# Moving the top three bits of a 64-bit weight's low word from a VectorE shift to a ScalarE byte read

## The chip, the cores and the metric

The kernel runs on one core of one Trainium2 chip. The metric is the device time of one execution in microseconds. Before the change the median of three runs is 1188.74 us (1188.38 to 1191.08). The engines are TensorE (PE; PEld is its weight load), VectorE (DVE), ScalarE (ACT), GpSimd (POOL) and SyncE (SP), which issues nearly all DMAs.

## The reference, cut to what matters

Windowed attention with memory tokens on 4 x 768 tokens, then two feed-forward layers on its 3072 x 512 output:

```python
# attention: chunks of 32 queries, 16 keys to the left, 8 to the right, 8 memory keys, 8 heads of 64
x = attention(q, k, v, mem_k, mem_v)          # (3072, 512)
# first layer: w_in 512 x 2048, w_out 2048 x 512
h = x @ w_in
P = a[0] + a[1]*h + a[2]*h**2 + a[3]*h**3
Q = 1 + abs(b[0])*abs(h) + abs(b[1])*h**2
x = (P / (Q + 1e-6)) @ w_out
# second layer: w1, w2 512 x 1024, w3 1024 x 1024, w_out 1024 x 512
return ((x @ w1) * (x @ w2) @ w3) @ w_out
```

All weights of the two layers arrive as 64-bit floats. A matmul here takes operands of a shorter format, so every weight and every activation is split into a high and a low part, and each product is made of three matmuls (high x high, high x low, low x high).

## The kernel before, in words

Tokens are processed in blocks of 384 (8 blocks). In the **first layer** a step n is one block and one of 16 slices of 128 hidden columns: twelve matmuls into a PSUM bank `h` (`gemm1`, three such banks), the rational function on ScalarE, VectorE and GpSimd (`rat_*`, lines 332 to 372), its split into `gh` (ScalarE) and `gl` (GpSimd, line 381), and twelve matmuls into four accumulators (`gemm2`). The last rational step, `rat_end` (line 372, VectorE), is what frees the bank `h`. Attention units of 64 queries run in between: scores on PE, softmax on VectorE, ScalarE and GpSimd (the normalisation, line 294), two more PE steps, and the split of the result into `xr`. The first six units, those of block 0, run before the first `gemm1`.

In the **second layer**, `gemm3` makes the two factors `ab` (w1 and w2, kept interleaved in `w12`), a gate multiplies and splits them, and w3 @ w_out is made once as eight products `w3o` (24 matmuls each), whose split results are the weights of `gemm4`. The eight `w3o` stand between the gated products of the first block.

**The decode.** Each of 72 weight chunks (128 x 512 values of 64 bits) is loaded into one of four buffers `raw`, as pairs of 32-bit words (low, high), and turned into a 32-bit float and its two parts by six steps (lines 204 to 240):

1. `load` (SP): the DMA, 512 KB.
2. `scale` (ScalarE, line 214): the high word, read as a float, times 2^-112, which moves its exponent to the 32-bit format's.
3. `low` (VectorE, line 218): the low word shifted right by 29, which leaves its top three bits.
4. `join`, twice (VectorE, line 222): the scaled word shifted left by three, or-ed with these bits; then or-ed with the sign.
5. `high_part` (ScalarE, line 226) into `wA` or `wB`, or into a buffer for w3.
6. `low_part` (GpSimd, line 229): the value less its high part. It and step 5 free the buffer.

32 chunks (w_in, w_out) are decoded in the ramp, that is until all slices of block 0 are done; 40 more (16 of w12, 8 of the second w_out, 16 of w3) from the last block of the first layer on, as their places come free.

**What sets the order.** Every step has a due time and, for each engine that may do it, a cost, both tables of numbers in the kernel (`R`, `DI`, `DO`, `DW`, `A0`, `AS`, `H0` and so on). A planner in the kernel (`order`, line 104) walks through a model of the engines and emits each engine's instructions in one fixed order; GpSimd's steps and those VectorE steps marked `port` never overlap in its model. On the chip every engine works in that order, and waits at the head of its queue for what the next instruction needs.

Of the kernel before, what the change touches and what calls it, by code (L numbers as in the profile page):

```python
# [26 lines left out]
NF1 = F1 // P  # L27
# [7 lines left out]
SIGN = -2 ** 31  # L35
# [3 lines left out]
def attention_rational_mlp_gated_mlp(  # L39
# [15 lines left out]
    pe, act, dve, pool, sp = nc.tensor, nc.scalar, nc.vector, nc.gpsimd, nc.sync  # L55
# [11 lines left out]
    wB = const.tile([P, NF1, 2, DM], F32R, name="wB")  # L67
# [6 lines left out]
    att = ExitStack()  # L74
# [7 lines left out]
    def bank(tag, name):  # L82
        return ps.tile([P, DM], F32, tag=tag, bufs=rings[tag], name=name)
# [111 lines left out]
    def raw(name):  # L195
        return rawp.tile([P, DM, 2], I32, tag="raw", name=name)

# [3 lines left out]

    def decode(t, src, dst, *ready, take=(), early=(), LOW=None):

        r, d = [], []

        def load():
            r.append(raw("w64"))
            sp.dma_start(out=r[0], in_=src.bitcast(I32).rearrange("p (k t) -> p k t", t=2))  # L210

        def scale():
            hi = r[0][:, :, 1].bitcast(F32)
            act.activation(out=hi, in_=hi, func=AF.Copy, scale=2.0 ** -112)  # L214

        def low():
            lo = r[0][:, :, 0]
            dve.tensor_scalar(out=lo, in0=lo, scalar1=29, scalar2=None, op0=ALU.logical_shift_right)  # L218

        def join(op, n):  # L220
            lo, hi = r[0][:, :, 0], r[0][:, :, 1]
            dve.scalar_tensor_tensor(out=lo, in0=hi, scalar=n, in1=lo, op0=op, op1=ALU.bitwise_or)  # L222

        def high_part():
            d.append(dst() if callable(dst) else dst)
            act.activation(out=d[0][:, 0], in_=r[0][:, :, 0].bitcast(F32), func=AF.Copy)

        def low_part(eng):
            eng.tensor_tensor(out=d[0][:, 1], in0=r[0][:, :, 0].bitcast(F32), in1=d[0][:, 0].bitcast(F32),  # L229
                              op=ALU.subtract)  # L230

        a = step(t, {"dma": 1.46}, load, *early, take=("raw",))
        b = step(t, {"act": 0.58}, scale, a)
        c = step(t, {"dve": 0.335}, low, a, port=True)
        c = step(t, {"dve": 0.602}, lambda: join(ALU.logical_shift_left, 3), b, c, port=True)
        c = step(t, {"dve": 0.602}, lambda: join(ALU.bitwise_and, SIGN), c, port=True)
        h = step(t + H0, {"act": 0.58}, high_part, c, *ready, take=take)
        l = step(t + H0, LOW or LOWA, low_part, h, frees=[a], port=True)
        a.until.append(h)
        return h, l  # L240

    def mm3(out_, w, wi, x, xi, first, last):

        for i, (a, c) in enumerate(((0, 0), (0, 1), (1, 0))):
            pe.matmul(out_, lhsT=wi(w, a), rhs=xi(x, c), start=first and i == 0, stop=last and i == 2)  # L245
# [185 lines left out]

    def w3o(i):

        o = w3os[i] = bank(("acc3", "att")[i % 2], "w3o")
        for jc in range(NF2):
            mm3(o, w3s[i, jc // 4], lambda w, a: w[:, a, jc % 4 * P:(jc % 4 + 1) * P], wB, lambda w, a: w[:, jc, a],
                jc == 0, jc == NF2 - 1)
# [52 lines left out]
    def wA_slot(f):  # L490
        return wA[:, f].rearrange("p a c k -> p a (c k)")

    def two(v, p, d):
        return {g: c for g, c in (("pool", p), ("dve", d)) if g[0] in v}

    PAIR7 = two('d', .551, .27); LOWB = two('p', 1.225, .602); GLO7 = two('p', .956, .469); GATE = two('p', .956, .469)
    LOWA, PAIR, GLO, XLO = two('p', 1.225, .602), two('p', .551, .27), two('p', .956, .469), two('d', 1.764, .87)
    H0 = 1.098
    FIN = {"act": 0.48, "dve": 0.6}

    def start():
# [8 lines left out]
    n1, n2 = NB * NF1, NB * NF2  # L510
    first = step(-99, {"none": 0.0}, start)
    G1, G2, VL = {}, {}, {}
    T0 = -9.693; UP = 0.781; A0 = -1.160; AS = 0.526


    lq, lv, s_, ex, tc_, v_ = ({-2: None, -1: None} for _ in range(6))
# [2 lines left out]
    def attend(u):  # L519
        blk, o = divmod(u, UPB)  # L520
        t = T0 + UP * u if blk == 0 else 8 / 3 * (u - UPB) + A0
        k = UP / 4 if blk == 0 else AS
# [16 lines left out]
        VL[u] = step(t + 1.55 * k, {"dve": 0.335}, lambda: v_parts(u, 1), vh, frees=[v_[u]])  # L539


    R = (0.00,0.64,0.28,0.40,0.44,0.36,0.64,0.52,0.83,0.81,1.11,1.39,1.21,1.59)
    DI, DO = -3.895, -2.305
    WI, WO = {}, {}
    chunks = sorted([(f + DI, 0, f) for f in range(NF1)] + [(f + LAG + 0.45 + DO, 1, f) for f in range(NF1)])
    SPL = {}

    def ffn1(n):
        blk, f = divmod(n, NF1)
        d = [VL[u] for u in range(blk * UPB, blk * UPB + UPB)] if f == 0 else [G1[n - 1]]  # L550
# [22 lines left out]

    for u in range(UPB):
        attend(u)
    for t, o, f in chunks:
        (WO if o else WI)[f] = decode(t, *((w_out[f], wB[:, f]) if o else (w_in[f], wA_slot(f))))
    u = UPB
    for n in range(n1):
        ffn1(n)  # L580
# [10 lines left out]
    sec = step(n1 - 16, {"none": 0.0}, second, *VL.values(), v_[NU - 1], tc_[NU - 1])  # L591
# [3 lines left out]
    tG = [n1 + m + 0.05 if m < LAG else TB + TG * (m - LAG) for m in range(NF2)]  # L595
    TW = TB + (NF2 - LAG) * TG + XB * TG
    tO = [TW + (TO + (TO + TM) * (i - 1) if i else 0) for i in range(NF2)]
    T1 = tO[-1] + TO
    PB = 1.23
    tG += [(TW + TG * (m - NF2 - XB) if m - NF2 < XB else T1 + PB * (m - NF2 - XB)) for m in range(NF2, n2)]  # L600
    DW, D3, DV = -2.122, -5.330, -1.521
    W12, WO2, W3, OP, G3, G4, X2 = {}, {}, {}, {}, {}, {}, {}
    for f in range(NF1):
        W12[f] = decode(tG[f // 2] + f % 2 * 0.4 + DW, w12[f], wA_slot(f), G1[n1 - NF1 + f], early=[G1[n1 - NF1 + max(0, f - 1)]], LOW={"dve": .602} if f < 0 else LOWB)
    for j in range(NF2):
        WO2[j] = decode(tO[0] + DV + 0.3 * j, w_out2[j], wB[:, j], G2[n1 - NF1 + j], early=[G2[n1 - NF1 + j]], LOW=LOWB)

    def x2(blk):
        t = tG[blk * NF2]
# [43 lines left out]
        gates[m] = ffn2_in(m)  # L653
    O = {}
    for i in range(NF2):
        W3[i] = [decode(tO[i] + 0.5 * g + D3, w3T[i, :, g], w3_dst(i, g), sec, take=("w3",), early=[sec] if i < 2 else [O[i - 2]], LOW=LOWB) for g in range(2)]
        t = tO[i]
        tag = ("acc3", "att")[i % 2]
        o = O[i] = step(t, {"pe": 5.61}, lambda i=i: w3o(i), *[x for p in W3[i] for x in p], *[x for p in WO2.values() for x in p],
                 G2[n1 - 1], *([G4[i - 2]] if i > 1 else []), take=(tag,), frees=[p[0] for p in W3[i]])  # L660
        d = []
        if i:
            ffn2_out(i - 1, t + TO)
            d = [G4[i - 1]]
# [78 lines left out]
```

## Time and profile before

| | |
|---|---|
| median of the runs | 1188.74 us |
| profiled execution, its own time | 1193.64 us |
| its span | 1191.8 us |
| PE busy | 1121.2 us (94%) |
| VectorE busy | 668.2 us (56%) |
| ScalarE busy | 667.0 us (56%) |
| GpSimd busy | 476.4 us (40%) |
| mean granted TensorE clock | 0.983 |

The profile is of one execution; its own time is the span plus what lies around it. Busy shares are averages over the whole: the page's slices and the tables by stage show where PE is not full, and the lists of waits show what ended its idle time there. The granted clock is TensorE's, as a share of its full 2.4 GHz; its lower level is 1.2 GHz.

### The profile page before, as it was taken

What the parts mean: (1) busy time and instruction counts of PE and PEld (TensorE: products, weight loads), DVE (VectorE), ACT (ScalarE), POOL (GpSimd) and SP (SyncE); (2) the same over time, 40 slices, a digit from 0 to 9 for tenths busy, and PEclk for the clock granted to TensorE, in tenths of its full rate; (3) what the DMA queues carried; (4) which work ended last, traced back from release to release, by engine and by line L of the source; (5) the groups of instructions that cost most, each with busy time, mean ns of one, the idle gap of its engine ahead of it and who ended that gap; (6) DMA issues with size and microseconds to landing.
All of it is one profiled execution on the core that took longest, in us unless ns stands there. A gap on an engine that the chain in (4) does not pass through costs nothing.

```text
span 1191.8 us, 18531 instructions
## 1 busy us (share of the span) xinstructions
PE 1121.2 (94%) x7104; PEld 1042.2 (87%) x7104; DVE 668.2 (56%) x1249; ACT 667.0 (56%) x1267; POOL 476.4 (40%) x444
## 2 busy tenths in 40 slices
PE   5587699999999999999999799989999999999998
PEld 4476589999999999999999699978889999999997
DVE  6799896667776677676767878855301010110100
ACT  4576687777787777777777866543312222222121
POOL 2466665444444444444444556633211111111111
PEclk9988799999999999999999999989999999999999
DMA  8535322121121121211220232643101101011000
GB/s 241 153 89 167 107 89 63 37 69 37 47 63 36 43 66 44 62 37 43 74 95 1 76 123 84 210 137 107 36 27 54 53 1 53 1 53 54 1 27 27
DMA packets 28028, 83.07 MB, mean 70 GB/s; under 512 B 3746, under 2 KB 3874, under 8 KB 27938
## 3 DMA queue, kind: packets, MB, share of 16 engines
q1 hardware_dynamic: 27648, 81.80, 22.1%
q8 instruction: 56, 0.92, 0.3%
q14 instruction: 32, 0.26, 0.1%
q10 hardware_dynamic: 292, 0.09, 0.0%
HBM read 69.30 MB, written 12.58 MB: 69 GB/s over the span
## 4 chain that ended last, share of the span: by engine, by line
PE 76%; DVE 7%; DMA 5%; ACT 5%; POOL 4%; issue 3%; SPq 0%; POOLq 0%; DVEq 0%; ACTq 0%
PE acc L245 28%; PE ab L245 19%; PE h L245 18%; PE w3o L245 4%; PE sc L262 3%; DVE w L222 2%; DMA w<-in_w_dram 2%; PE xo L308 2%; POOL wA L229 2%; DMA w<-in_w_in_dram 2%; DMA w<-in_w_out_dram 2%; PE at L299 1%; DVE w L218 1%; POOL wB L229 1%; ACT A L334 1%
## 5 line engine op out<-in xcount | busy, mean ns | idle before, releaser
L245 PE MATMUL h<-xr,wA 128*128 128x384 f32 x1536 | 308.7, 351 | 27.9 <-DVE A L372 26.7
L245 PEld LDWEIGHTS h<-xr,wA 128*128 128x128 f32 x1536 | 277.6, 195 | 35.6 <-DVE A L372 30.8
L245 PE MATMUL acc<-gh,wB 128*128 128x384 f32 x1024 | 287.4, 343 | 1.5 <-POOL wB L229 1.5
L245 PE MATMUL ab<-xr,wA 128*128 128x384 f32 x1536 | 280.1, 337 | 5.0 <-DVE W L460 4.5
L245 PEld LDWEIGHTS ab<-xr,wA 128*128 128x128 f32 x1536 | 271.2, 189 | 10.8 <-DVE W L460 5.1
L346 POOL TENSOR_TENSOR W<-W,Q 128x384 f32<-128x384 f32 x128 | 132.9, 1038 | 211.1 <-ACT Q L342 172.6
L460 DVE TENSOR_TENSOR W<-W,ab 128x384 f32<-128x384 f32 x64 | 35.4, 553 | 288.7 <-PE ab L245 287.5
L245 PEld LDWEIGHTS acc<-gh,wB 128*128 128x128 f32 x1024 | 186.2, 188 | 7.4 <-POOL wB L229 2.3
L245 PE MATMUL acc<-gl,wB 128*128 128x384 f32 x512 | 171.7, 335 | 0.0
L469 POOL TENSOR_TENSOR gl<-W,gh 128x384 fp32r<-128x384 f32 x56 | 56.8, 1016 | 280.4 <-ACT gh L464 280.4
L381 POOL TENSOR_TENSOR gl<-A,gh 128x384 fp32r<-128x384 f32 x128 | 136.7, 1069 | 41.1 <-ACT gh L376 33.9
L364 DVE SCALAR_TENSOR_TENSOR A<-A,cf,h 128x384 f32<-128x384 f32 x128 | 78.0, 609 | 102.4 <-ACT h L360 101.8
L222 DVE SCALAR_TENSOR_TENSOR w<-w 128x512 int32<-128x512 int32 x144 | 119.7, 854 | 5.9 <-ACT w L214 5.3
L456 ACT COPY W<-ab 128x384 f32<-128x384 f32 x64 | 30.7, 480 | 142.8 <-PE ab L245 142.8
L334 ACT ACTIVATE A<-h,cf 128x384 f32<-128x384 f32 x128 | 85.5, 668 | 43.0 <-PE h L245 42.3
L358 ACT ACTIVATE Q<-W,one 128x384 f32<-128x384 f32 x128 | 78.9, 616 | 41.0 <-POOL W L346 40.5
L245 PEld LDWEIGHTS acc<-gl,wB 128*128 128x128 f32 x512 | 96.4, 188 | 0.0
L464 ACT CAST gh<-W 128x384 fp32r<-128x384 f32 x56 | 28.7, 512 | 117.2 <-DVE W L460 110.7
L342 ACT ACTIVATE Q<-W,cf 128x384 f32<-128x384 f32 x128 | 90.8, 709 | 4.0
L245 PE MATMUL acc<-wB,gh 128*128 128x512 f32 x294 | 92.2, 394 | 0.0
L351 DVE TENSOR_TENSOR A<-A,h 128x384 f32<-128x384 f32 x128 | 70.1, 548 | 15.9 <-ACT W L334 14.2
L353 DVE SCALAR_TENSOR_TENSOR A<-A,cf,h 128x384 f32<-128x384 f32 x128 | 77.7, 607 | 2.3 <-ACT W L334 0.6
(61 smaller groups left out, 1401.4 us busy)
## 6 DMA issues: line engine op xcount, KB each, us to landing
qk<-in_qkT_dram SPq DMA_DIRECT2D x48, 320.0 KB, 3.9
w<-in_w_out_dram SPq DMA_DIRECT2D x24, 512.0 KB, 4.5
v<-in_vW_dram SPq DMA_DIRECT2D x48, 192.0 KB, 2.4
w<-in_w_in_dram SPq DMA_DIRECT2D x16, 512.0 KB, 4.8
w<-in_w3T_dram SPq DMA_DIRECT2D x16, 512.0 KB, 3.8
w<-in_w_dram SPq DMA_DIRECT2D x16, 512.0 KB, 4.5
x2d<-x2o SPq DMA_DIRECT2D x16, 384.0 KB, 2.7
x<-x2d SPq DMA_DIRECT2D x16, 384.0 KB, 4.1
```

The lines of the kernel that those rows point to most:

```text
L222: dve.scalar_tensor_tensor(out=lo, in0=hi, scalar=n, in1=lo, op0=op, op1=ALU.bitwise_or)
L229: eng.tensor_tensor(out=d[0][:, 1], in0=r[0][:, :, 0].bitcast(F32), in1=d[0][:, 0].bitcast(F32), op=ALU.subtract)
L245: pe.matmul(out_, lhsT=wi(w, a), rhs=xi(x, c), start=first and i == 0, stop=last and i == 2)
L334: act.activation(out=t, in_=hps[n][src], func=func, scale=scale, bias=bias)
L342: act.activation(out=t, in_=hps[n]["W"], func=AF.Identity, scale=cf[:, 5:6], bias=cf[:, 4:5])
L346: pool.tensor_tensor(out=W, in0=W, in1=Q, op=ALU.mult)
L351: dve.tensor_tensor(out=A, in0=A, in1=h, op=ALU.mult)
L353: dve.scalar_tensor_tensor(out=A, in0=A, scalar=cf[:, 1:2], in1=h, op0=ALU.add, op1=ALU.mult)
L358: act.activation(out=Q, in_=W, func=AF.Ln, bias=one)
L364: dve.scalar_tensor_tensor(out=A, in0=A, scalar=cf[:, 0:1], in1=r, op0=ALU.add, op1=ALU.mult)
L381: eng.tensor_tensor(out=gl, in0=hps.pop(n)["A"], in1=gt[n].bitcast(F32), op=ALU.subtract)
L469: eng.tensor_tensor(out=gl, in0=hps.pop(m), in1=gt[m].bitcast(F32), op=ALU.subtract)
```

## The change

In `decode`, step 3 can be done by ScalarE (`byte=True`): it reads only the top byte of the low word (one byte out of every eight), multiplies by 1/32, subtracts 0.484375 and writes an integer, whose rounding gives the same three bits. All 32 chunks of the ramp do this (`BYTE`), and every second one of the 40 later ones (`BYTT`). `w3o` puts all eight products into the bank `acc3` instead of alternating between `acc3` and `att`. Some due times are other numbers. The new arguments `tag`, `TAGS`, `TAGT` (a PSUM bank for the scaled word) are `None` everywhere, so nothing goes that way, and `LOWS`, `LOWT` name the same engine as before.

```diff
-        def low():
+        def low(eng):
             lo = r[0][:, :, 0]
-            dve.tensor_scalar(out=lo, in0=lo, scalar1=29, scalar2=None, op0=ALU.logical_shift_right)
+            if eng is act:
+                top = r[0].bitcast(U8).rearrange("p k (t b) -> p k t b", b=4)[:, :, 0, 3]
+                act.activation(out=lo, in_=top, func=AF.Copy, scale=1.0 / 32, bias=-0.484375)
+            else:
+                dve.tensor_scalar(out=lo, in0=lo, scalar1=29, scalar2=None, op0=ALU.logical_shift_right)
...
-        c = step(t, {"dve": 0.335}, low, a, port=True)
+        c = step(t, {"act": 0.58} if byte else {"dve": 0.335}, low, a, port=not byte)
...
-        o = w3os[i] = bank(("acc3", "att")[i % 2], "w3o")
+        o = w3os[i] = bank("acc3", "w3o")
...
-    H0 = 1.098
+    H0 = 1.034
+    TAGS, BYTE, LOWS = (None,), (True,), (LOWA,)
+    TAGT, BYTT, LOWT = (None,), (False, True), (LOWA,)
...
-    T0 = -9.693; UP = 0.781; A0 = -1.160; AS = 0.526
+    T0 = -9.693; UP = 0.781; A0 = -1.044; AS = 0.832
...
-    DI, DO = -3.895, -2.305
+    DI, DO = -4.925, -2.305
...
-    DW, D3, DV = -2.122, -5.330, -1.521
+    DW, D3, DV = -1.654, -5.330, -1.521
```

In `R`, the due time of `rat_slope` goes from 0.28 to 0.20. What stands in each engine's queue shows what moves.

VectorE in the ramp, in front of the `rat_end` (A<-h,A) of the first slice, for which the fourth `gemm1` waits; `w_...` are the decode's buffers, `e` and `r` the softmax's. Before:

```order
L353 SCALAR_TENSOR_TENSOR A<-A,cf,h 128x384
L276 TENSOR_TENSOR e_84<-sc,mx 128x384
L222 SCALAR_TENSOR_TENSOR w_409<-w_409 128x512
L218 TENSOR_SCALAR w_413<-w_413 128x512
L218 TENSOR_SCALAR w_418<-w_418 128x512
L284 TENSOR_REDUCE sm<-e_84 128x4
L364 SCALAR_TENSOR_TENSOR A<-A,cf,h 128x384
L288 TENSOR_SCALAR r<-sm 128x4
L289 RECIPROCAL r<-r 128x4
L368 SCALAR_TENSOR_TENSOR h<-W,one,h 128x384
L351 TENSOR_TENSOR A<-A,h 128x384
L372 SCALAR_TENSOR_TENSOR A<-h,A 128x384
```

After:

```order
L370 SCALAR_TENSOR_TENSOR A<-A,cf,h 128x384
L293 TENSOR_TENSOR e_84<-sc,mx 128x384
L233 SCALAR_TENSOR_TENSOR w_412<-w_412 128x512
L301 TENSOR_REDUCE sm<-e_84 128x4
L381 SCALAR_TENSOR_TENSOR A<-A,cf,h 128x384
L305 TENSOR_SCALAR r<-sm 128x4
L306 RECIPROCAL r<-r 128x4
L385 SCALAR_TENSOR_TENSOR h<-W,one,h 128x384
L368 TENSOR_TENSOR A<-A,h 128x384
L389 SCALAR_TENSOR_TENSOR A<-h,A 128x384
```

The two shifts (L218) are gone from the row; the rest stands as it stood.

ScalarE at the same place, from the chunks ahead of the first rational step to that step's logarithm (Q<-W,one). Before:

```order
L214 ACTIVATE w_390<-w_390 128x512
L214 ACTIVATE w_409<-w_409 128x512
L334 ACTIVATE A<-h,cf 128x384
L334 ACTIVATE W<-h 128x384
L342 ACTIVATE Q<-W,cf 128x384
L214 ACTIVATE w_413<-w_413 128x512
L214 ACTIVATE w_418<-w_418 128x512
L226 ACTIVATE wA<-w_390 128x512
L358 ACTIVATE Q<-W,one 128x384
```

After:

```order
L220 ACTIVATE w_412<-w_412 128x512
L226 ACTIVATE w_412<-w_412 128x512
L351 ACTIVATE A<-h,cf 128x384
L351 ACTIVATE W<-h 128x384
L359 ACTIVATE Q<-W,cf 128x384
L243 ACTIVATE wA<-w_390 128x512
L220 ACTIVATE w_423<-w_423 128x512
L226 ACTIVATE w_423<-w_423 128x512
L375 ACTIVATE Q<-W,one 128x384
```

L220 is now the scale step and L226 the byte read: each chunk has the two in a row, and one chunk stands where two stood.

PE around the first `w3o`; `spare` and `wB` on the right of `acc` are the split results of `w3o`, `acc` a `gemm4`. Before:

```order
L245 MATMUL ab<-xr,wA 128x384 x228
L245 MATMUL w3o<-wB,w_7145 128x512 x12
L245 MATMUL w3o<-wB,w_7243 128x512 x12
L245 MATMUL w3o<-wB,w_7403 128x512 x12
L245 MATMUL w3o<-wB,w_8053 128x512 x12
L245 MATMUL acc<-spare,wB 128x512 x9
L245 MATMUL ab<-xr,wA 128x384 x24
L245 MATMUL w3o<-wB,w_8521 128x512 x12
```

After:

```order
L262 MATMUL ab<-xr,wA 128x384 x204
L262 MATMUL w3o<-wB,w_7144 128x512 x12
L262 MATMUL w3o<-wB,w_7195 128x512 x12
L262 MATMUL ab<-xr,wA 128x384 x12
L262 MATMUL w3o<-wB,w_7385 128x512 x12
L262 MATMUL w3o<-wB,w_7943 128x512 x12
L262 MATMUL acc<-spare,wB 128x512 x9
L262 MATMUL ab<-xr,wA 128x384 x12
```

The first `w3o` stands two gated products (24 matmuls) earlier, and one gated product now follows each `w3o` or `gemm4` before the next `w3o`. From the end of block 0 to the last block of the first layer, every engine's order is the same as before.

## Rows read from the trace of the kernel before

**Rows 1.** The page's 40 slices, busy share in tenths: TensorE and ScalarE.

```profile
PE   5587699999999999999999799989999999999998
...
ACT  4576687777787777777777866543312222222121
```

**Rows 2.** Stages: busy us of PE, PEld, DVE, ACT, POOL; PEclk, DMA share, GB/s.

```profile
0.00:42.60 42.60, 21.63 (x216) 16.96 (x216) 31.22 (x62) 18.84 (x36) 15.59 (x17) 1.00 0.72 196
42.60:100.00 57.40, 44.46 (x296) 39.54 (x296) 48.66 (x92) 44.13 (x83) 32.28 (x29) 0.91 0.46 138
100.00:175.00 75.00, 58.65 (x375) 52.93 (x376) 68.62 (x120) 51.40 (x96) 50.22 (x39) 0.86 0.37 116
...
640.00:781.00 141.00, 124.33 (x704) 120.67 (x702) 117.03 (x180) 98.91 (x188) 83.95 (x69) 0.98 0.34 110
```

**Rows 3.** Waits from 0 to 180 us: who for whom, us, times, longest.

```profile
ACT wA L226 <- DVE w L222: 17.6, 10, 2.9
...
PE h L245 <- DVE A L372: 15.0, 7, 4.9
...
PE at L299 <- POOL e L294: 10.5, 5, 5.1
```

**Rows 4.** Line 218 alone by stage: DVE busy us, PEclk, DMA share, GB/s.

```profile
0.00:42.60 42.60, 8.02 (x8) 1.00 0.72 196
42.60:100.00 57.40, 6.34 (x9) 0.91 0.46 138
100.00:175.00 75.00, 11.62 (x16) 0.86 0.37 116
```

**Rows 5.** One line's instructions, whole span: duration in ns, min/median/max.

```profile
L218 DVE TENSOR_SCALAR w<-w x72: 414/428/1552, 9.8 to 846.2; 128x512 int32<-128x512 int32 x72
...
L214 ACT ACTIVATE w<-w x72: 651/679/708, 9.8 to 845.4; 128x512 f32<-128x512 f32 x72
...
L222 DVE SCALAR_TENSOR_TENSOR w<-w x144: 660/684/1817, 11.4 to 847.8; 128x512 int32<-128x512 int32 x144
...
L229 POOL TENSOR_TENSOR wA<-w,wA x32: 1292/1322/1872, 15.2 to 761.0; 128x512 fp32r<-128x512 f32 x32
```

**Rows 6.** Groups from 100 to 175 us, the joins and GpSimd: busy, mean ns.

```profile
L222 DVE SCALAR_TENSOR_TENSOR w<-w 128x512 int32<-128x512 int32 x32 | 27.4, 884 | 0.3 <-ACT w L214 0.3
...
L229 POOL TENSOR_TENSOR wB<-w,wB 128x512 fp32r<-128x512 f32 x11 | 18.4, 1676 | 10.3 <-ACT wB L226 10.3
L346 POOL TENSOR_TENSOR W<-W,Q 128x384 f32<-128x384 f32 x10 | 11.9, 1188 | 3.3 <-ACT Q L342 3.3
L381 POOL TENSOR_TENSOR gl<-A,gh 128x384 fp32r<-128x384 f32 x10 | 11.9, 1186 | 2.4 <-ACT gh L376 2.4
L229 POOL TENSOR_TENSOR wA<-w,wA 128x512 fp32r<-128x512 f32 x5 | 7.3, 1456 | 6.2 <-ACT wA L226 6.2
L294 POOL TENSOR_TENSOR e<-e,r 128x384 f32<-128x384 f32 x3 | 2.8, 925 | 3.8 <-ACT h L360 3.1 <-DVE r L289 0.6
```

**Rows 7.** The same groups of GpSimd, 175 to 640 us.

```profile
L381 POOL TENSOR_TENSOR gl<-A,gh 128x384 fp32r<-128x384 f32 x94 | 95.8, 1019 | 19.7 <-ACT gh L376 18.4 <-issue 1.1
L346 POOL TENSOR_TENSOR W<-W,Q 128x384 f32<-128x384 f32 x93 | 94.5, 1017 | 176.8 <-ACT Q L342 138.5 <-PE acc L245 21.8 <-PE xo L308 16.5
L294 POOL TENSOR_TENSOR e<-e,r 128x384 f32<-128x384 f32 x35 | 29.0, 829 | 51.4 <-DVE r L289 51.4
```

**Rows 8.** Two short stretches of the transition, columns as in rows 2.

```profile
663.00:672.00 9.00, 4.76 (x24) 4.12 (x24) 8.07 (x14) 8.80 (x18) 7.54 (x7) 1.00 0.19 54
...
776.00:781.00 5.00, 0.91 (x6) 0.58 (x5) 5.00 (x7) 2.35 (x5) 2.28 (x3) 0.89 0.54 133
```

**Rows 9.** Lines 442 and 444; last, a piece of the chain (start, us).

```profile
L442 ACT ACTIVATE wB<-w3o x7: 597/599/599, 809.5 to 859.7; 128x512 fp32r<-128x512 f32 x7
...
L444 DVE TENSOR_TENSOR wB<-w3o,wB x7: 691/691/692, 810.1 to 860.3; 128x512 fp32r<-128x512 f32 x7
...
864.03 2.11 PE ab L245 x12
```

More of the change, by code (lines that the diff above doesn't have):

```diff
@@ L10 @@
 I32 = mybir.dt.int32
+U8 = mybir.dt.uint8
 AF = mybir.ActivationFunctionType
@@ L199, in raw32, with decode @@
         return raw(name).rearrange("p k t -> p (k t)").bitcast(F32)
-    def decode(t, src, dst, *ready, take=(), early=(), LOW=None):
-        r, d = [], []
+    def decode(t, src, dst, *ready, take=(), early=(), LOW=None, tag=None, byte=False):
+        r, d, b = [], [], []
+        LOW = LOW or LOWA
+        inps = tag and "pool" not in LOW
         def load():
@@ L213, in scale @@
             hi = r[0][:, :, 1].bitcast(F32)
-            act.activation(out=hi, in_=hi, func=AF.Copy, scale=2.0 ** -112)
-        def low():
+            b.append(bank(tag, "wx") if tag else hi)
+            act.activation(out=b[0], in_=hi, func=AF.Copy, scale=2.0 ** -112)
+        def low(eng):
             lo = r[0][:, :, 0]
-            dve.tensor_scalar(out=lo, in0=lo, scalar1=29, scalar2=None, op0=ALU.logical_shift_right)
-        def join(op, n):
-            lo, hi = r[0][:, :, 0], r[0][:, :, 1]
-            dve.scalar_tensor_tensor(out=lo, in0=hi, scalar=n, in1=lo, op0=op, op1=ALU.bitwise_or)
+            if eng is act:
[3 more added lines that the diff above has]
+                dve.tensor_scalar(out=lo, in0=lo, scalar1=29, scalar2=None, op0=ALU.logical_shift_right)
@@ new lines, in join, with value @@
+        def join(i):
+            lo, hi, x = r[0][:, :, 0], r[0][:, :, 1], b[0].bitcast(I32)
+            if i == 0:
+                dve.scalar_tensor_tensor(out=x if tag else lo, in0=x, scalar=3, in1=lo, op0=ALU.logical_shift_left, op1=ALU.bitwise_or)
+            else:
+                dve.scalar_tensor_tensor(out=x if inps else lo, in0=hi, scalar=SIGN, in1=x if tag else lo, op0=ALU.bitwise_and,
+                                         op1=ALU.bitwise_or)
+        def value():
+            return b[0] if inps else r[0][:, :, 0].bitcast(F32)
@@ L224, in high_part @@
         def high_part():
             d.append(dst() if callable(dst) else dst)
-            act.activation(out=d[0][:, 0], in_=r[0][:, :, 0].bitcast(F32), func=AF.Copy)
+            act.activation(out=d[0][:, 0], in_=value(), func=AF.Copy)
         def low_part(eng):
-            eng.tensor_tensor(out=d[0][:, 1], in0=r[0][:, :, 0].bitcast(F32), in1=d[0][:, 0].bitcast(F32),
-                              op=ALU.subtract)
+            eng.tensor_tensor(out=d[0][:, 1], in0=value(), in1=d[0][:, 0].bitcast(F32), op=ALU.subtract)
@@ L232, in decode @@
         a = step(t, {"dma": 1.46}, load, *early, take=("raw",))
-        b = step(t, {"act": 0.58}, scale, a)
-        c = step(t, {"dve": 0.335}, low, a, port=True)
-        c = step(t, {"dve": 0.602}, lambda: join(ALU.logical_shift_left, 3), b, c, port=True)
-        c = step(t, {"dve": 0.602}, lambda: join(ALU.bitwise_and, SIGN), c, port=True)
+        s = step(t, {"act": 0.58}, scale, a, take=(tag,) if tag else ())
+        c = step(t, {"act": 0.58} if byte else {"dve": 0.335}, low, a, port=not byte)
@@ L237, in decode @@
+        J = {"dve": 0.64 if tag else 0.602}
+        c = step(t, J, lambda: join(0), s, c, port=not tag)
+        c = step(t, J, lambda: join(1), c, frees=[a] if inps else [s], port=not tag)
         h = step(t + H0, {"act": 0.58}, high_part, c, *ready, take=take)
-        l = step(t + H0, LOW or LOWA, low_part, h, frees=[a], port=True)
-        a.until.append(h)
+        l = step(t + H0, LOW, low_part, h, frees=[s] if inps else [a], port=not inps)
+        (s if inps else a).until.append(h)
         return h, l
@@ L494, in two @@
         return {g: c for g, c in (("pool", p), ("dve", d)) if g[0] in v}
-    PAIR7 = two('d', .551, .27); LOWB = two('p', 1.225, .602); GLO7 = two('p', .956, .469); GATE = two('p', .956, .469)
-    LOWA, PAIR, GLO, XLO = two('p', 1.225, .602), two('p', .551, .27), two('p', .956, .469), two('d', 1.764, .87)
-    H0 = 1.098
+    PAIR7 = two('d', .551, .27); LOWB = two('p', 1.225, .64); GLO7 = two('p', .956, .469); GATE = two('p', .956, .469)
+    LOWA, PAIR, GLO, XLO = two('p', 1.225, .64), two('p', .551, .27), two('p', .956, .469), two('d', 1.764, .87)
+    H0 = 1.034
+    TAGS, BYTE, LOWS = (None,), (True,), (LOWA,)
+    TAGT, BYTT, LOWT = (None,), (False, True), (LOWA,)
     FIN = {"act": 0.48, "dve": 0.6}
@@ L539, in attend @@
         VL[u] = step(t + 1.55 * k, {"dve": 0.335}, lambda: v_parts(u, 1), vh, frees=[v_[u]])
-    R = (0.00,0.64,0.28,0.40,0.44,0.36,0.64,0.52,0.83,0.81,1.11,1.39,1.21,1.59)
-    DI, DO = -3.895, -2.305
+    R = (0.00,0.64,0.20,0.40,0.44,0.36,0.64,0.52,0.83,0.81,1.11,1.39,1.21,1.59)
+    DI, DO = -4.925, -2.305
     WI, WO = {}, {}
@@ L575, in attention_rational_mlp_gated_mlp @@
         attend(u)
-    for t, o, f in chunks:
-        (WO if o else WI)[f] = decode(t, *((w_out[f], wB[:, f]) if o else (w_in[f], wA_slot(f))))
+    for k, (t, o, f) in enumerate(chunks):
+        (WO if o else WI)[f] = decode(t, *((w_out[f], wB[:, f]) if o else (w_in[f], wA_slot(f))), tag=TAGS[k % len(TAGS)], byte=BYTE[k % len(BYTE)], LOW=LOWS[k % len(LOWS)])
     u = UPB
@@ L600, in attention_rational_mlp_gated_mlp @@
     tG += [(TW + TG * (m - NF2 - XB) if m - NF2 < XB else T1 + PB * (m - NF2 - XB)) for m in range(NF2, n2)]
-    DW, D3, DV = -2.122, -5.330, -1.521
+    DW, D3, DV = -1.654, -5.330, -1.521
     W12, WO2, W3, OP, G3, G4, X2 = {}, {}, {}, {}, {}, {}, {}
     for f in range(NF1):
-        W12[f] = decode(tG[f // 2] + f % 2 * 0.4 + DW, w12[f], wA_slot(f), G1[n1 - NF1 + f], early=[G1[n1 - NF1 + max(0, f - 1)]], LOW={"dve": .602} if f < 0 else LOWB)
+        W12[f] = decode(tG[f // 2] + f % 2 * 0.4 + DW, w12[f], wA_slot(f), G1[n1 - NF1 + f], early=[G1[n1 - NF1 + max(0, f - 1)]], LOW=LOWT[f % len(LOWT)], tag=TAGT[f % len(TAGT)], byte=BYTT[f % len(BYTT)])
     for j in range(NF2):
-        WO2[j] = decode(tO[0] + DV + 0.3 * j, w_out2[j], wB[:, j], G2[n1 - NF1 + j], early=[G2[n1 - NF1 + j]], LOW=LOWB)
+        WO2[j] = decode(tO[0] + DV + 0.3 * j, w_out2[j], wB[:, j], G2[n1 - NF1 + j], early=[G2[n1 - NF1 + j]], LOW=LOWT[j % len(LOWT)], tag=TAGT[j % len(TAGT)], byte=BYTT[j % len(BYTT)])
     def x2(blk):
@@ L655, in attention_rational_mlp_gated_mlp @@
     for i in range(NF2):
-        W3[i] = [decode(tO[i] + 0.5 * g + D3, w3T[i, :, g], w3_dst(i, g), sec, take=("w3",), early=[sec] if i < 2 else [O[i - 2]], LOW=LOWB) for g in range(2)]
+        W3[i] = [decode(tO[i] + 0.5 * g + D3, w3T[i, :, g], w3_dst(i, g), sec, take=("w3",), early=[sec] if i < 2 else [O[i - 2]], LOW=LOWT[g % len(LOWT)], tag=TAGT[g % len(TAGT)], byte=BYTT[g % len(BYTT)]) for g in range(2)]
         t = tO[i]
-        tag = ("acc3", "att")[i % 2]
         o = O[i] = step(t, {"pe": 5.61}, lambda i=i: w3o(i), *[x for p in W3[i] for x in p], *[x for p in WO2.values() for x in p],
-                 G2[n1 - 1], *([G4[i - 2]] if i > 1 else []), take=(tag,), frees=[p[0] for p in W3[i]])
+                 G2[n1 - 1], *([G4[i - 2]] if i > 1 else []), take=("acc3",), frees=[p[0] for p in W3[i]])
         d = []
```

## The prediction

> **What bounds the kernel now.** I read the page's slices first [rows 1]. PE stands at 9 tenths or more in all but two places: the first six slices (0 to about 175 us), and a stretch from about 640 to 790 us. Wherever PE is full, a VectorE or ScalarE saving is worth nothing, so only these two places can move the time. The stages [rows 2] put numbers on them. Before the first w_in product (0 to 42.6 us) PE has only attention work. From 42.6 to 100 us it is busy 44.46 of 57.4 us (idle 12.9), from 100 to 175 us 58.65 of 75.0 (idle 16.4), from 640 to 781 us 124.33 of 141.0 (idle 16.7). In the same two ramp stages its mean granted clock is 0.91 and 0.86: after some waits the first product runs at the lower level (1.2 GHz), so a wait that goes can give back a little more than itself.
>
> Next, who lets PE wait [rows 3]. Until 180 us the longest releaser is the VectorE step at L372: the last rational step, which frees the PSUM bank that the next w_in product needs. It held PE for 15.0 us in 7 waits; POOL's softmax normalisation (itself behind VectorE's reciprocal) held it for 10.5 us in 5. So PE waits for a **queue on VectorE**, and in that queue stand the decode's integer steps: L218 (shift) and L222 (two joins), three per weight chunk, 32 chunks in the ramp.
>
> Then what those steps cost. The shift takes 428 ns at the median but up to 1552 [rows 5]; by stage its mean is 1.00, 0.70 and 0.73 us [rows 4]. The joins have a median of 684 ns, a mean of 0.884 between 100 and 175 us [rows 5, 6]. POOL's own steps stretch there too: 1.676 and 1.456 us for the low parts of weights against a median of 1.322 [rows 5, 6], 1.19 against 1.02 for the rational step and the low part of g [rows 6, 7]. Both engines lengthen each other, as if they took turns at something they share. Summed at undisturbed durations between 100 and 175 us: POOL 16 x 1.322 + 10 x 1.017 + 10 x 1.019 + 3 x 0.829 = 44.0 us; VectorE 16 x 0.428 + 32 x 0.684 = 28.7 us. Together 72.7 of 75.0 us. If these steps exclude one another, **that shared thing is full (97%)** and sets the pace of this stage; VectorE, busy 68.6, shows mostly its symptom.
>
> The Trainium skill (GPSIMD Engine Reference, Key points) says that GpSimd shares its SBUF interfaces with VectorE and that contention arises with VectorE instructions in a 2-port mode or with two SBUF inputs. The rows above agree, and by that rule the joins (two SBUF inputs) go on colliding after the shift is gone.
>
> **The change part by part.**
>
> *The shift leaves VectorE, a byte read comes onto ScalarE.* This is done in all 32 chunks of the ramp and in 20 of the later 40. Off VectorE: one L218. Onto ScalarE: one activation of 512 elements, which no row shows with a one-byte input. The nearest is the scale step L214, same length, same 8-byte step, 651 to 708 ns, median 679 [rows 5]. I take 0.68 and no gain or loss from the byte type. It stands behind L214 of its own chunk, so scale and low bits, which ran side by side on two engines, become 1.36 us in a row before the first join.
>
> *0 to 42.6 us.* Eight shifts, 8.02 us of VectorE [rows 4], 3.4 at the median. ScalarE gets 8 x 0.68 = 5.4 us on 18.84 [rows 2]: it has room. The chain of a chunk grows by 0.68; with four load buffers eight chunks are two rounds, +1.4. Ends: -6.6 (all of 8.02 less 1.4) and +1.4. I take **-2**, the median price less 1.4.
>
> *42.6 to 100 us.* Nine shifts: 3.9 us at the median, 6.34 as seen. ScalarE goes from 44.13 to 50.3 us of 57.4, 88%, more than VectorE's 48.66 less 3.9 to 6.3. The load only changes engines. I take **0**, ends -3.9 and +6.2 (every byte read on the path).
>
> *100 to 175 us.* Sixteen shifts: 11.62 us of VectorE as seen, 16 x 0.428 = 6.8 us of the shared time. ScalarE goes from 51.40 to 62.3 us (83%). If the shared thing stays at 97%, the stage needs (72.7 - 6.8) / 0.97 = 67.9 us, 7.1 less. Ends: -11.6 and 0 (the joins and ScalarE take up what is freed). I take **-6**, near the row of the shared sum, less about one us for the longer chain.
>
> *640 to 796 us.* Half the chunks change. In places ScalarE is the full one (8.80 of 9.0 us while PE did 4.76), in others VectorE (5.00 of 5.0 us, PE 0.91) [rows 8], so the same edit costs at the first and pays at the second. ScalarE's sum would be at most 98.9 + 20 x 0.68 = 112.5 of 141 us, VectorE's less than its 117.0 [rows 2]. I take **0**; ends -4.1 (the VectorE stall at 776 to 781) and +4.
>
> *w3 @ w_out2 in one bank.* Its eight products took turns between two banks; now each must wait until the one before is copied out: one ScalarE and one VectorE step, 0.60 + 0.69 us [rows 9]. Between two of them the new order puts a gated product of 2.1 us [rows 9], which covers these 1.3 us. If that cover were gone, 7 x 1.3 = 9 us; but PE is full in that stretch and the product is in the order, so I take 0. The first of the eight now stands two gated products (4.2 us) earlier. Where the weights that it needs are not decoded sooner, PE waits there, but has those two products left to do: the loss is in the +4 above.
>
> *Other step order.* The order on all engines from about 190 to 640 us is the old one, so it costs nothing. On SP a few loads of attention and of weights change places in the ramp; the first four weight loads stand where they stood, and the ends of the first stage cover the rest. The end of the kernel is unchanged.
>
> **Sum:** -2 + 0 - 6 + 0 = -8 us. The profiled execution took 1193.64 us (span 1191.8), 4.9 above the median of the three runs; I take the difference as it is to the median: 1188.74 - 8 = 1180.7 us. PE's work is unchanged, and idle time won in the ramp is not lost again, since PE is full from 175 to 640 us.
>
> **The rivals.**
>
> *ScalarE becomes the bound (slower).* From 42.6 to 175 us its load rises from 95.5 to 112.6 us of 132.4, so the break-even lies at a busy share of **85%**. Below it the stage grows. For it: before, no slice of the ramp shows ScalarE above 8 tenths [rows 1], its chain alternates with two other engines, and at 663 to 672 us PE waits while ScalarE is full [rows 8]. At 82% the two stages need 137.3 us, +4.9: **1193.6 us**. Against it: it was held back by VectorE itself (17.6 us waiting for the joins before one kind of step [rows 3]), and no step of ScalarE stretches under contention.
>
> The Trainium skill (ScalarE: Activation LUTs, Rules for kernel authors) tells authors to use VectorE, not ScalarE, for plain adds and multiplies. By that rule this move is the wrong way round; its result would be this rival's. Undisturbed, the rows agree (428 against 679 ns); in the ramp they do not (0.70 to 1.00 us as seen).
>
> *The waiting moves to the joins (no change).* The wait in L218 was for POOL, and the join behind it meets the same POOL step. Then VectorE wins 0.43 us a chunk, POOL nothing, and the chain's extra 0.68 takes most of it back: -2 us, **1186.7 us**. For it: a join also reaches far above its median. Against it: the shared sum itself falls by 6.8 us, wherever the waits stand.
>
> *The whole of L218 counts.* If all of 8.02 + 6.34 + 11.62 us as seen went from PE's path, less 1.4 and with half lost to ScalarE, -12.3: **1176.4 us**.
>
> **How the numbers follow.** A measurement of this kernel tells about 0.3% (3.6 us) from no change. Forecast (1178 to 1185) 0.52; whole L218 0.08; waiting moves to the joins 0.22; ScalarE bound 0.18. So faster 0.60, within 0.3% 0.22, slower 0.18. For 8 in 10 the range runs from 1174 (beyond the third rival, and the low ends of the first two stages) to 1193.5 (the first rival at 82%), leaving out its worse half.
>
> **What would show it.** Right: PE's share between 100 and 175 us rises above 0.85, the waits for L372 fall well below 15 us, the joins' mean there stays at or below 0.88, the byte read takes 0.66 to 0.71 us, and PE is full some 8 us earlier. Wrong: joins with a mean near 1.1 us (second rival); or ScalarE above 85% from 42.6 us on with PE waiting at L372 as long as before (first rival); or a PE gap in front of the first w3 @ w_out2 product longer than 4 us.

## The result and the profile after

The changed kernel takes **1173.49 us** (median of four runs, 1170.22 to 1174.35) against 1189.25 beside it: ratio 0.986, 95% interval 0.9837 to 0.9883. Timed once more on another occasion it was 0.984 (0.9818 to 0.9862). That is some 16 to 19 us faster; the forecast was 8, and the range ended at 1174.0. The direction was right, the size was off by a factor of two.

The span of the profiled execution is 1172.3 us. The page's 40 slices of PE and ScalarE:

```profile
PE   5678899999999999999999799999999999999998
...
ACT  5798897777777777877778887644222222122221
```

The slices of rows 1 now read 5 6 7 8 instead of 5 5 8 7 6 at the start, and PE is full one slice earlier. The stages, columns as in [rows 2], to be read against them:

```profile
42.60:100.00 57.40, 44.86 (x305) 40.86 (x304) 48.87 (x85) 48.91 (x93) 34.39 (x31) 0.88 0.46 133
100.00:175.00 75.00, 65.19 (x451) 59.83 (x450) 64.84 (x118) 68.12 (x132) 50.30 (x44) 0.91 0.39 118
...
640.00:781.00 141.00, 131.48 (x711) 127.10 (x710) 107.02 (x161) 104.03 (x195) 87.70 (x71) 0.96 0.41 133
```

Between 100 and 175 us PE went from 58.65 to 65.19 us and ScalarE from 51.40 to 68.12 (91%); VectorE fell only from 68.62 to 64.84. Between 640 and 781 us PE went from 124.33 to 131.48. The waits of PE until 180 us, against [rows 3] (15.0 and 10.5 us):

```profile
PE h L262 <- DVE A L389: 11.6, 6, 3.5
...
PE at L316 <- POOL e L311: 1.1, 2, 0.9
```

The byte read and the two joins of the changed kernel, by source (ns, min/median/max) and by group until 175 us (busy us, mean ns):

```profile
L226 ACT ACTIVATE w<-w x52: 642/666/732, 10.3 to 828.4; 128x512 int32<-128x512 uint8 x52
```

```profile
L235 DVE SCALAR_TENSOR_TENSOR w<-w 128x512 int32<-128x512 int32 x32 | 31.5, 996 | 0.1
L233 DVE SCALAR_TENSOR_TENSOR w<-w 128x512 int32<-128x512 int32 x32 | 31.1, 987 | 6.2 <-ACT w L226 6.2
```

The byte read costs what was assumed (666 ns). The joins (lines 233 and 235) got longer; the same groups of before, both joins in one line and then the shift, were:

```profile
L222 DVE SCALAR_TENSOR_TENSOR w<-w 128x512 int32<-128x512 int32 x63 | 50.7, 830 | 0.3 <-ACT w L214 0.3
L218 DVE TENSOR_SCALAR w<-w 128x512 int32<-128x512 int32 x32 | 26.0, 826 | 6.9 <-DMA w<-in_w_in_dram 5.5 <-DMA w<-in_w_out_dram 1.3
```

To place the gain I use one mark in all traces: the start of the last of the 48 attention products `xo`, which stands in the last part of the stretch where PE is full. What comes before it is the ramp and the full stretch, whose order is the same in all kernels here (but for a few steps at its edges); what comes after it holds the transition. Before, then after (start, length, us):

```profile
640.36 0.69 PE L308 MATMUL xo<-aT,v 96*64 96x64 f32 x16
```

```profile
628.24 0.69 PE L325 MATMUL xo<-aT,v 96*64 96x64 f32 x16
```

So the first w_in product starts 3.6 us earlier (39.06 for 42.62), the mark 12.1 us, and from the mark to the end of the span it is 551.44 before and 544.06 after, 7.4 us less. These are two single executions; the one of before took 1193.64 us against its median of 1189.25, so the two pieces add up to 19.5 and not to 16. The second profile of the changed kernel has its mark at 629.36 and 544.34 us behind it.

### The profile page after: what moved, and what is told of

It is laid out like the page before. It is cut to its first block, busy times and chain, and to the rows that moved or that the text cites. A ratio compares the mean times of both kernels' runs of the same rounds, so it can differ in the third digit from the quotient of the medians.

```text
span 1172.3 us, 18507 instructions
## 1 busy us (share of the span) xinstructions
PE 1119.6 (96%) x7104; PEld 1042.3 (89%) x7104; DVE 647.3 (55%) x1197; ACT 694.7 (59%) x1319; POOL 474.5 (40%) x444
## 4 chain that ended last, share of the span: by engine, by line
PE 78%; DVE 9%; ACT 4%; DMA 3%; POOL 3%; issue 3%; POOLq 0%; DVEq 0%; ACTq 0%
PE acc L262 30%; PE ab L262 19%; PE h L262 19%; PE w3o L262 4%; PE sc L279 3%; DVE w L233 2%; PE xo L325 2%; DVE w L235 2%; PE at L316 1%; POOL wA L246 1%; DMA w<-in_w_dram 1%; DVE h L385 1%; DMA qk<-in_qkT_dram 1%; DVE A L368 1%; DMA w<-in_w_out_dram 1%
## 5 line engine op out<-in xcount | busy, mean ns | idle before, releaser
L262 PE MATMUL acc<-gh,wB 128*128 128x384 f32 x1024 | 290.4, 346 | 1.1 <-POOL wB L246 1.1
L262 PEld LDWEIGHTS acc<-gh,wB 128*128 128x128 f32 x1024 | 188.8, 190 | 6.8 <-POOL wB L246 1.7
L481 ACT CAST gh<-W 128x384 fp32r<-128x384 f32 x56 | 28.7, 512 | 115.9 <-DVE W L477 111.1
L368 DVE TENSOR_TENSOR A<-A,h 128x384 f32<-128x384 f32 x128 | 70.2, 548 | 15.8 <-ACT W L351 14.4
L385 DVE SCALAR_TENSOR_TENSOR h<-W,one,h 128x384 f32<-128x384 f32 x128 | 78.5, 614 | 0.3
```

Of the source, the lines that this page charges most:

```text
L368: dve.tensor_tensor(out=A, in0=A, in1=h, op=ALU.mult)
L385: dve.scalar_tensor_tensor(out=r, in0=W, scalar=one, in1=r, op0=ALU.add, op1=ALU.mult)
```

## Experiments

A "mark" below is the start of that last attention product, "rest" the span less the mark. All ratios are to the kernel before, run beside each; beside the experiments it took 1191.69 to 1192.92 us, 2 to 4 more than in the result, so ratios compare better than times. Executions of one kernel differ by some 0.3%, so a mark of one profile is good to about 2 us.

### Which part pays: the engine put back, with the order kept

The order of every other instruction stays as the changed kernel's planner made it; only the engine of the step is the old one, in the ramp (shown) or, with `if byte and not ramp`, in the later chunks.

```diff
-        c = step(t, {"act": 0.58} if byte else {"dve": 0.335}, low, a, port=not byte)
+        c = step(t, {"act": 0.58} if byte else {"dve": 0.335}, (lambda: low(dve)) if ramp else low, a, port=not byte)
```

> The changed kernel with its planned order of all steps kept as it is, but in the 32 chunks of the ramp the low bits are made by the VectorE shift again, at the place in the order where the ScalarE byte read stood. Theory A (VectorE and what it shares with GpSimd were the bound, so the engine of this step is what pays): most of the ramp's gain goes, 1182 to 1187 us against 1173.5. Theory B (the new order and numbers pay, whichever engine makes the bits): within 3 us of 1173.5.

Measured: 1180.0 us, 0.9911 (0.9892 to 0.9929). Between the two theories: the mark moves from 628.24 back to 633.40, 5 of the 12 us. The first w_in product still starts at 39.44 us. So what the shift costs on VectorE is real, but the larger part of the ramp's gain survives its return.

> The changed kernel with its order kept, but the 20 byte reads of the later chunks are VectorE shifts again. The trace puts about 7 us of the gain behind 628 us, where the forecast had 0. Theory A: the 20 shifts less on VectorE made it, 1177 to 1181 us. Theory B (step order and one bank for w3 @ w_out2 made it): within 3 us of 1173.5.

Measured: 1177.79 us, 0.9887 (0.987 to 0.9904). In Theory A's range: the rest grows from 544.06 to 548.53, the mark stays (627.37). The interval of the ratio touches the changed kernel's, so the reading leans on the rest.

### New numbers without the byte read, and the byte read with the old numbers

`BYTE` and `BYTT` to `(False,)` in the first; the old due times and the two banks in the second.

> The changed kernel with no byte read at all (every chunk by the VectorE shift, planned so), that is the new due times and the one bank alone. Theory A: within 4 us of the kernel before (1189). Theory B: most of the gain, 1174 to 1179 us.

Measured: 1196.2 us, 1.0044 (1.0028 to 1.0059): slower than before, by just more than the 4 us that Theory A allowed. Mark 643.63, rest 551.97. The due times and the one bank give nothing by themselves.

> The kernel before (its due times, its two banks for w3 @ w_out2) with the byte read in the same chunks as the changed kernel, planned anew. Theory A: 1173 to 1179 us. Theory B: 1184 to 1190 us.

Measured: 1175.72 us, 0.9868 (0.9849 to 0.9887): nearly all of the gain, with mark 628.95. So it is the byte read, planned as such, that pays, and hardly the numbers. Its rest is 547.75, against 543 to 546 in the profiles that have the new numbers and the changed kernel's later chunks, so some 2 to 4 us behind the mark may be theirs.

### The engine alone and the order alone

These two separate what the run above holds together. `engine_only` keeps the order that the planner made for the kernel before and only has ScalarE do the step; `order_only` has the planner believe in the byte read and lets VectorE do the shift.

```diff
# engine_only
+        c = step(t, {"dve": 0.335}, (lambda: low(act)) if byte else (lambda: low(dve)), a, port=True)
# order_only
+        c = step(t, {"act": 0.58} if byte else {"dve": 0.335}, lambda: low(dve), a, port=not byte)
```

> The kernel before, its order of all other steps, its numbers and two banks kept, with the 52 low-bit steps of the changed kernel done by the ScalarE byte read at the place in the order where the shift stood. Theory A (the engine pays, the order little): 1176 to 1181 us. Theory C (engine and order pay about half each, as the shift put back in the ramp suggests: 5 us of 12): 1181 to 1185 us. If the old order makes ScalarE wait at the wrong places: 1186 or more.

Measured: 1192.5 us, **1.0001** (0.9985 to 1.0016). Nothing. Mark 639.95, as before. The joins until 175 us:

```profile
L233 DVE SCALAR_TENSOR_TENSOR w<-w 128x512 int32<-128x512 int32 x32 | 30.3, 950 | 15.4 <-ACT w L226 14.4 <-ACT w L220 0.9
L235 DVE SCALAR_TENSOR_TENSOR w<-w 128x512 int32<-128x512 int32 x31 | 29.5, 959 | 0.4
```

All engines in the same stretch, before and then in this run (columns as in [rows 2], third value VectorE):

```profile
0.00:175.00 175.00, 124.74 (x887) 109.43 (x888) 148.51 (x271) 114.38 (x215) 98.09 (x84) 0.91 0.48 142
```

```profile
0.00:175.00 175.00, 128.37 (x892) 112.82 (x893) 133.58 (x240) 130.84 (x248) 94.56 (x84) 0.92 0.49 144
```

VectorE no longer does 26.0 us of shifts, but its idle time rises from 26.5 to 41.4 us, 14.9 more: it now stands 14.4 us in front of the first joins until a byte read is done, where before it stood 6.9 us in front of the shifts until a load had landed, and it waits longer for other ScalarE steps too. The joins themselves last 0.950 and 0.959 us instead of 0.830: 63 x 0.125 = 7.9 us more. Together some 23 of the 26.0 us are gone again on VectorE itself.

> The kernel before with its numbers and two banks, planned as if the 52 steps were ScalarE byte reads, but all done by the VectorE shift: the order alone. Theory A: 1186 to 1192 us. Theory C: 1181 to 1185 us, the first w_in product at about 39.5 us instead of 42.6.

Measured: 1186.72 us, 0.9936 (0.9913 to 0.996): some 6 to 8 us. The time is in Theory A's range, but that was set for a kernel before at 1189; against the 1192.92 beside it, it lies between Theory A and C. The first w_in product stands at 40.71 us. The order alone gives about half, the engine alone nothing, both together 0.9868. The two do not add. By the marks (us):

| old due times | mark | rest |
|---|---|---|
| before | 640.36 | 551.44 |
| `engine_only` | 639.95 | 547.55 |
| `order_only` | 638.12 | 547.88 |
| both (`byte_old_numbers`) | 628.95 | 547.75 |

It is in the ramp that each needs the other: alone they move the mark by 0.4 and 2.2 us, which one profile hardly tells from nothing, together by 11.4. Behind the mark either alone comes as far as both, some 4 us. That the whole time of `engine_only` is still that of before is not settled by its profile: that execution was 3.2 us shorter than the median of its runs. Under the new due times `shift_back_ramp` kept 7 of the 12 us, more than the 2.2 of 11.4 here, so what the order is worth by itself hangs on the due times too.

> As engine_only (the kernel before, its order and numbers kept, 52 byte reads on ScalarE), but each byte read stands right behind the scale step of its own chunk instead of where the shift stood. In engine_only VectorE sat idle 14.4 us before joins until a byte read. Theory D (that run lost its gain to the place of the byte read): 1178 to 1183 us, that idle time under 5 us. Theory E (the whole order of the ramp, loads and joins and not this place alone, has to change with the engine): 1188 to 1193 us.

```diff
# engine_only, and:
             act.activation(out=b[0], in_=hi, func=AF.Copy, scale=2.0 ** -112)
+            if byte:
+                low(act)
```

(The step at the old place is left empty.) Measured: 1191.83 us, 0.9999 (0.9987 to 1.0011), in Theory E's range. The place of the byte read in ScalarE's queue is not what the old order lacked: the idle time before the first join fell from 15.4 to 9.3 us and nothing came of it.

```profile
L237 DVE SCALAR_TENSOR_TENSOR w<-w 128x512 int32<-128x512 int32 x32 | 28.1, 887 | 0.4
...
L235 DVE SCALAR_TENSOR_TENSOR w<-w 128x512 int32<-128x512 int32 x32 | 28.7, 906 | 9.3 <-ACT w L228 9.3
```

What in the order matters beyond that was not taken apart further; that it is the order as a whole, as Theory E says, is what is left over and not shown.

### What the shift took: VectorE's time, or what it shares with GpSimd

The changed kernel with one more VectorE step per chunk of the ramp, in front of the first join, order kept: in the first a shift by zero in place, in the second a reduction of equal length.

```diff
+                    dve.tensor_scalar(out=lo, in0=lo, scalar1=0, scalar2=None, op0=ALU.logical_shift_right)
# or
+                    dve.tensor_reduce(out=scr, in_=b[0][:, :270], op=ALU.max, axis=AX.X)
```

> The changed kernel, order kept, with one more VectorE step per chunk of the ramp in front of its first join: a shift by zero in place, the same instruction as the old shift (428 ns undisturbed, up to 1550 beside GpSimd). Theory P (what VectorE shares with GpSimd is what was full): costs 6 to 10 us, and clearly more than the next run. Theory V (VectorE's own time is what counts): 4 to 7 us, as the next run.

> The changed kernel, order kept, with one more VectorE step per chunk of the ramp at the same place, of the same undisturbed length, but of a kind that never stretches in the trace (a reduction of 270 elements from one SBUF operand, about 0.43 us; the softmax's reduction of 384 takes 535 to 556 ns in all 48 cases). Theory P: under half of what the run before costs. Theory V: the same, 4 to 7 us.

Measured: the shift 1187.06 us, 0.9969 (0.9949 to 0.999); the reduction 1180.41 us, 0.9904 (0.987 to 0.9938). Against the changed kernel's 0.984 to 0.986 that is 13 to 15 us and 5 to 8 us. The two steps in their traces (ns, min/median/max):

```profile
L234 DVE TENSOR_SCALAR w<-w x32: 410/428/1248, 11.2 to 169.3; 128x512 int32<-128x512 int32 x32
```

```profile
L235 DVE TENSOR_REDUCE scr<-w x32: 403/426/434, 10.5 to 159.3; 128x1 f32<-128x270 f32 x32
```

Equal at the median, but the shift reaches 1248 ns and the reduction never passes 434. So 32 x 0.43 = 13.7 us more of VectorE's own time cost 5 to 8 us, and the same 13.7 us of a step that collides with GpSimd cost about twice that; the shift cost more than either theory allowed. Whether the reduction cost under half of it (Theory P) the intervals do not decide. The two runs stand 7 to 8 us apart, and until 175 us VectorE was busy with the shifts for 21.6 us and with the reductions for 13.6: **both** count, VectorE's own time, and about as much again for what it shares with GpSimd. One more thing differs, since the shift has to wait for the byte read and the reduction only for the scale step; but the idle time in front of these steps and the first joins is 4.2 us with the shift and 3.5 with the reduction, so this explains under one us.

> The changed kernel, order kept, with one more ScalarE step of 0.68 us per chunk of the ramp (the scaled word copied onto itself), 21.8 us in all. ScalarE is now busy 68.1 of 75.0 us between 100 and 175 us. If ScalarE has become the bound of the ramp: 14 to 22 us slower than 1173.5. If it still has room: under 7 us.

```diff
+            if ramp:
+                act.activation(out=b[0], in_=b[0], func=AF.Copy, scale=1.0)
```

Measured: 1179.15 us, 0.9901 (0.9873 to 0.9928): 21.8 us of ScalarE work cost 5 to 7 us, as expected of an engine with room. ScalarE is at 92 and 96% in the two ramp stages of that run and still not the bound:

```profile
42.60:100.00 57.40, 45.53 (x293) 41.60 (x292) 47.85 (x79) 52.57 (x98) 32.76 (x28) 0.88 0.45 128
100.00:175.00 75.00, 61.19 (x405) 56.07 (x404) 64.08 (x116) 72.15 (x135) 48.68 (x43) 0.91 0.40 113
```

The two lines are 42.6 to 100 and 100 to 175 us, columns as in [rows 2].

### One bank, and the split between ramp and later chunks

> The changed kernel with w3 @ w_out2 in two banks in turn again, planned anew. If the one bank costs or gives nothing (TensorE is full there in both): within 3 us of 1173.5. If the one bank and the gated products between them made part of the gain behind 628 us: 1176 to 1179 us.

Measured: 1174.57 us, 0.9856 (0.9832 to 0.9881). The bank is worth nothing that can be measured.

> The changed kernel with the byte read in the ramp alone (later chunks by the shift, planned so; its numbers and one bank kept). If the later byte reads pay what the order-held run showed (4 us): 1177 to 1181 us. If they pay nothing once the order is planned for the shift: 1172 to 1176 us.

Measured: 1179.19 us, 0.9901 (0.9879 to 0.9922). Mark 625.58, rest 551.42. In the first of its two ranges: the later byte reads pay.

> The changed kernel with the byte read in every second later chunk alone, the ramp by the shift, planned so. With numbers_alone at 1.0044 of before and 4 to 7 us for the later part: 1187 to 1193 us.

Measured: 1191.07 us, 0.9992 (0.9972 to 1.0012), within what was expected. Mark 647.00, rest 544.00. Put together with `numbers_alone` (643.63, 551.97) the four combinations agree: the byte reads of the ramp move the mark by 18 to 19 us under the new numbers (which by themselves make the ramp some 3 us longer), those of the later chunks shorten the rest by 7 to 8 us, and neither clearly changes the other's.

### Other shares of the byte read

> The changed kernel with all 40 later chunks by the byte read instead of every second one, planned anew. If VectorE's queue still bounds the transition: 1169 to 1172 us. If ScalarE, which was full there for 9 us at a time in the trace of before, is now the bound: 1175 us or more.

`BYTT` to `(True,)`. Measured: 1177.63 us, 0.9873 (0.9848 to 0.9899). In the second range. The rest goes from 544.1 to 549.7: with all later chunks on ScalarE most of the later gain is lost. PE waits 4.94 us in front of a gated product again, now for a ScalarE step (line 473).

> The changed kernel with the byte read in two of three chunks of the ramp, planned so. Extra work on ScalarE cost a quarter of its length and on VectorE half or all of it, so if loads alone decide, every shift put back costs: 1177 to 1181 us. If a better balance pays: under 1172 us.

`BYTE` to `(True, True, False)`. Measured: 1177.84 us, 0.9889 (0.9866 to 0.9912). Within the first expectation. No run here beats the changed kernel.

> The changed kernel unchanged, timed beside the next three and the same runs of before: 0.984 to 0.988 of before. It is the measure for the others of this chip.

Measured: 1174.62 us, 0.984, as expected.

## Why the forecast was half the gain

**What failed.** Two steps of the sum. From 640 to 796 us the forecast let the stall of VectorE at 776 to 781 us (-4.1) cancel against +4 for places with ScalarE full, and took 0; the +4 did not come, and all behind the mark got 7.4 us shorter. And in the ramp the engine was priced by itself, with no term for the new step order: "Other step order" says "costs nothing" of 190 to 640 us, and looks in the ramp only at loads. Measured by the mark, the engine alone gives next to nothing there (0.4 us), and with its order 12.1 us came instead of 8.

**What bounds the kernel: right.** The gain came only where PE was not full, and out of the waits named: L372 (L389 after) fell from 15.0 to 11.6 us, the softmax normalisation from 10.5 to 1.1 [rows 3]. The second was named as a wait, but no term of the sum was made of it. (The first slices below nine tenths are five, to about 149 us, and not six.)

**0 to 42.6 us: -2 forecast, -3.6 measured.** Size nearly right, by luck: the reason was wrong. The forecast took the median price of eight shifts. With the engine alone changed the first w_in product stands at 42.36 us, with the shift put back into the new order at 39.44. It was mostly the order of the steps before that product, for which the forecast had no term.

**42.6 to 175 us: 0 and -6 forecast, about -8.5 measured** (the mark's 12.1 less the 3.6). The sum of what VectorE and GpSimd share was the right thing to look at: an extra step that collides costs about twice what one costs that does not. But it was treated as a budget that pays out whatever the order, and `engine_only` shows that it does not: 26.0 us of shifts off VectorE, and some 23 us of them come back as idle time and as longer joins. The order was only looked at for what it might cost. That the same planner, told that the step uses another engine, also stops keeping it clear of GpSimd (`port=not byte`) and can place loads and joins otherwise, was not counted as a gain. Without the new order the engine gains next to nothing in the ramp; which of these changes of order does it, no run shows.

**640 us to the end: 0 forecast, -7.4 measured; the largest miss.** The forecast named the right stall: VectorE full at 776 to 781 us [rows 8]. It is a wait of PE in front of a gated product, for VectorE's gate step (line 460, 477 after), and it goes away. Before, then after (in brackets the wait, us):

```profile
780.96 15.41 PE L245 MATMUL ab<-xr,wA 128*128 128x384 f32 x72 [4.09 <-DVE W L460]
```

```profile
768.01 4.44 PE L262 MATMUL ab<-xr,wA 128*128 128x384 f32 x24 [0.29 <-DVE W L477]
```

This wait is 4.0 to 4.1 us in the three profiles whose later chunks were neither planned nor run with the byte read (before, `numbers_alone`, `ramp_byte_alone`) and 3.56 in `byte_behind_scale`, and these four have a rest of 551 to 552; in every other profile the longest wait for that step is 2.3 us or less and the rest is shorter. What was set against it did not come: where ScalarE was full and PE busy for 4.76 of 9.0 us, PE is busy for 5.43 after. And the longer stretch between the two was not weighed. Below, 700 to 740 us before, and the places of 663 to 672 and 700 to 740 us after, 12.12 us earlier as the mark is (columns as in [rows 2]):

```profile
700.00:740.00 40.00, 36.73 (x208) 35.64 (x207) 39.21 (x62) 28.65 (x54) 25.74 (x21) 1.00 0.25 79
```

```profile
650.88:659.88 9.00, 5.43 (x23) 5.11 (x24) 8.73 (x13) 8.57 (x18) 6.73 (x6) 0.87 0.17 66
687.88:727.88 40.00, 39.10 (x223) 38.33 (x222) 35.16 (x54) 33.63 (x62) 27.08 (x22) 1.00 0.30 93
```

VectorE was busy 39.2 of 40 us there and ScalarE 28.7, and PE stood for 3.3 us; after, for 0.9. From the mark to the first w3 @ w_out2 product PE's idle time sums to 16.7 us before and 9.5 after: 7.2 of the 7.4 us. With the order kept, 20 byte reads in the later chunks are worth 4.5 us; planned for themselves, 7 to 8 us (`late_byte_alone`). The first w3 @ w_out2 product, for which the decode of that part has to be done, starts 24 us earlier (772.29 for 796.20), of which 12 are the ramp's; of the other 12, two gated products (4.2 us) had only moved behind it. That half of the chunks is the right share was not foreseen either: all of them on ScalarE lose most of it.

**The bank:** 0 forecast, nothing measured.

**Rival 1, ScalarE as the bound:** false. ScalarE rose to 91% between 100 and 175 us, and to 88% over both ramp stages, past the 85% at which it was to decide, so by its own condition the stages had to shrink; and 21.8 us more on it cost only 5 to 7. That ScalarE never stood above 8 tenths before said nothing on what it can reach. The Trainium skill's rule to use VectorE, not ScalarE, for plain arithmetic (ScalarE: Activation LUTs, Rules for kernel authors) did not hold for the ramp once the order was made for the move: the byte read took 666 ns at the median, the shift 826 ns on average until 175 us. With the old order kept, the move gave nothing.

**Rival 2, the waiting moves to the joins:** partly true, and I had set it against the forecast instead of inside it. The joins rose from 0.830 to 0.99 us, 64 x 0.16 = 10 us of the 26.0. That the move pays all the same shows only in the new order. The rule of the Trainium skill (GPSIMD Engine Reference, Key points) that steps with two SBUF inputs collide as well agrees with the trace of before: 72 joins that met no GpSimd tensor step took 675 to 695 ns, the 72 that met one up to 1817.

**What was to show it:** PE's share of 100 to 175 us above 0.85: 0.87. Byte read 0.66 to 0.71: 0.666. Joins at or below 0.88: 0.91 there (26 of them, 23.7 us; 0.99 until 175 us), missed. Waits for L372 well below 15 us: 11.6, hardly. PE full 8 us earlier: 12. Of the signs of being wrong none came in full: the joins stayed under 1.1 us, the waits for L372 did not stay as long, and PE waited 0.29 us shortly before the first w3 @ w_out2 product.

## What to carry to other kernels

Where a planner or a scheduler sets the order, an engine change and the order that it brings are one change: pricing the moved step by itself gave half the gain here, and running it in the old order gave none. Price a stretch by what every engine of it does over its whole length, and do not cancel a stall that a row shows against a cost that is only feared. An engine that looks three quarters busy because another holds it back may have all the room that the move needs; add dummy work to it to find out.

## What the runs showed of the hardware that was not expected

A ScalarE activation that reads one byte out of eight and writes 32-bit integers takes what its 32-bit neighbour takes: 642 to 732 ns for 512 elements, median 666, against 679.

Whether a VectorE step collides with GpSimd hangs on its kind, not on its length. In the trace of before, the 36 shifts (one SBUF operand) that met no GpSimd tensor step took 414 to 432 ns, the 36 that met one up to 1552; the joins behave alike. Reductions of one SBUF operand do not stretch: the 13 of 270 elements that lay wholly beside GpSimd steps in `extra_alone` took 421 to 434 ns, and the softmax's 48 of 384 elements in the changed kernel stay within these bounds:

```profile
L301 DVE TENSOR_REDUCE sm<-e x48: 535/544/554, 8.7 to 622.6; 128x4 f32<-128x384 f32 x48
```
